# Values of four heads' keys as 64x64 tiles, in two orders, in an attention and gated-MLP kernel

## The chip, the cores and the metric

The kernel runs on one core of a Trainium2 chip. The core has TensorE for matrix products (PE in the profile, its weight loads PEld), VectorE (DVE), ScalarE (ACT) and GpSimd (POOL), each with an instruction queue of its own, and a queue for transfers, SP. Products accumulate in PSUM, everything else is kept in SBUF. The metric is the device time in microseconds; three runs of the kernel before gave a median of 664.06 us (663.80 to 664.94).

## The reference

Eight batches, twelve heads, 448 positions, 64 values a head; the MLP is 768 wide, with 1024 hidden values.

```python
scores = scale * np.matmul(q, k.transpose(0, 1, 3, 2)) - np.log(S)
attn = 1.0 / (1.0 + np.exp(-scores))          # a sigmoid, no sum over keys
x = np.matmul(attn, v)                        # heads side by side: [8, 448, 768]
h = np.maximum(x @ w_in, 0.0)
u, v = h[..., :512], h[..., 512:]
v_n = (v - mean(v)) / sqrt(var(v) + 1e-6)
v_s = einsum('ts,bsd->btd', w_spatial, v_n) + b_spatial[None, :, None]
out = (u * v_s) @ w_out
```

Everything is float32. The kernel makes most products from two halves, a rounded high part and the rest (three products in place of one). The products of the attention with v are made with plain float32 operands, for which the trace shows two matmul instructions each.

## The kernel before

A *unit* is two heads of one batch: 48 units, 12 for each of four passes. A pass `m` (two batches) computes the attention of its units and then the MLP for both batches: gate values `pv` (`gate_values`), spatial products `pg`, hidden values `pu` (`gated`), outputs `po` (`output`). `in_program_order` fixes the order of each engine's instructions to that in which the code emits them, so an instruction that waits holds everything behind it on its engine or queue.

Attention goes by pairs of units, and, from the third pair of pass 0 on, by groups of four units `n` to `n + 3` (`attention_by_fours`): two groups in pass 0, three in each later pass, eleven in all. The 448 keys of a unit are three full tiles of 128 and a short one of 64; the short tiles of two units share one tile. `full` lists the twelve full tiles as (i, t): unit `n + i`, key tile t. Units 0 and 1 of a group write one pair's output, units 2 and 3 the second pair's.

In a group, `score_products` computes each tile's scores into a PSUM place (`banks`: four places of two banks, taken in turn; a score tile's place is that of the fourth one before). A ScalarE sigmoid takes the scores to SBUF; for the tiles in `by_vector`, (0,0), (1,0) and (2,0), a VectorE copy takes them, and ScalarE turns them in place later. Between the tiles the code emits what the next groups need: q/k loads (`attention_loads`), v loads (`value_loads`), and the split of q/k into high and low parts (`attention_splits`: a cast, on ScalarE in pass 0 and on VectorE later, and a VectorE subtraction).

In pass 0 `load_weights(n)` emits the next `n` steps of a generator that loads weights and splits them, mostly on VectorE: ten blocks for the gate and the spatial products must be done when the first gate product needs them. The last three steps make block 5 of `w_g_s`, which the sixth part of each gate product reads. The fours of pass 0 emit 7 steps in the first group and 9 in the second.

Then come the values. `value_products` multiplies a v tile of 128 keys x 64 (weights) with 128 x 448 attention values; the two heads of a unit run side by side, as two 128x64 tiles of the array. The short tiles run as four 64x64 tiles: rows 0 to 63 hold one unit's keys, rows 64 to 127 the other's. The first pair's output leaves PSUM by a ScalarE cast (high part) and a VectorE subtraction (`split_values`, lines 109 and 110). The second pair's is copied by ScalarE to a buffer (line 664), from where VectorE casts it and later subtracts (`lows`, `subtract_lows`). After the values come the short scores of the next group's pairs (line 293).

The buffers: `big` has seven for attention tiles, `vn` and some `gs`; `v` has two, which the v tiles and the second pair's copy share; `tmp` has three.

Of the kernel before, what the change touches and what calls it, by code (L numbers as in the profile page):

```python
# [14 lines left out]
P = 128  # L15
# [20 lines left out]
def attn_gmlp_kernel(  # L36
# [65 lines left out]
    nc.vector.memset(mhalf, -0.5)  # L102

    table = const.tile([P, 1], F32, name="table")
    shift(3 * 32, 2)
    nc.scalar.activation(table, bias_s, AF.Sigmoid)

    def split(hi, lo, src, copy):
        copy(hi, src)  # L109
# [3 lines left out]
        return ps_2.tile([P, 2, 512], F32, tag="ps2", name=name)  # L113


    BIG = 7

    BOUND = 122879.9921875
    SCALE = 2.0**-112
# [166 lines left out]
    def score_products(b, hp, t):  # L286
# [30 lines left out]
                    )  # L317
        return psc[:, :, :S]

    def room(b, hp, t, tag="big"):  # L320
        return work.tile(
            [P, 2, 512], F32, tag=tag, name=f"at_{b}_{hp}_{t}", bufs=BIG if tag == "big" else 3
        )[:, :, :S]

    def attention_scores(b, hp, t):
        psc = score_products(b, hp, t)
# [34 lines left out]
    def attention_values(b, hp, ats, direct):  # L361
        pav = banks(f"pav_{b}_{hp}")
        full = [t for t in range(TILES) if t != NFULL]
        for t in sorted(full, key=lambda t: copied(b, hp, t)) + [NFULL]:
            value_products(pav, b, hp, t, ats(t), start=t in (0, NFULL + 1))
        if direct:
            split_values(pav, b, hp)
        else:
            x = x_of(b, hp)
            xf = work.tile([P, 2, 512], F32, tag="big", name=f"x_{b}_{hp}", bufs=BIG)[:, :, :S]  # L370
# [9 lines left out]

    def warm_up():

        zeros = work.tile([P, 2, 512], F32, tag="big", name="zeros", bufs=BIG)[:, 0, :256]
# [13 lines left out]
    def gate_values(m, ts):  # L397

        n = len(ts)
        pv = banks(f"pv_{m}_{ts[0]}")  # L400
        for i, t in enumerate(ts):
            product(
                pv[:, i, :F],
                [
                    (
                        lambda a, cc=cc, t=t: x_s[:, a, cc, t * P : (t + 1) * P],
                        lambda c, cc=cc: w_g_s[:, cc, c, :],
                    )
                    for cc in range(NCC)
                ],  # L410
            )
        if n > 1:
            load_weights(1 if ts[0] else 5)
        rv = work.tile([P, 2, 512], F32, tag="tmp", name=f"rv_{m}_{ts[0]}", bufs=3)
        nc.scalar.activation(rv[:, :n], pv[:, :n], AF.Relu)  # L415
        mv = work.tile([P, 2, 2], F32, tag="mv", name=f"mv_{m}_{ts[0]}")
        for i in range(n):
            stats = work.tile([P, 6], F32, tag="stats", name=f"stats_{m}_{ts[i]}")
            nc.vector.bn_stats(stats, rv[:, i])  # L419
            nc.vector.bn_aggr(mv[:, i], stats)  # L420
        rstd = work.tile([P, 2], F32, tag="rstd", name=f"rstd_{m}_{ts[0]}")
        nc.gpsimd.tensor_scalar_add(rstd[:, :n], mv[:, :n, 1], 1e-6)
        nc.gpsimd.tensor_tensor(rstd[:, :n], rstd[:, :n], mhalf[:, :n], op=ALU.pow)
        for i in range(n):
            nc.vector.tensor_scalar_sub(rv[:, i], rv[:, i], mv[:, i, 0:1])
        load_weights(n - 1)
        for i, t in enumerate(ts):
            vn = work.tile([P, 2, 512], F32R, tag="big", name=f"vn_{m}_{t}", bufs=BIG)
# [16 lines left out]
            vns[t] = vn  # L445
        if n == 1:
            load_weights(1)
# [62 lines left out]
    def gated(b, fcs):  # L510
# [16 lines left out]
        load_weights(2)  # L527
        nc.vector.scalar_tensor_tensor(g, pu[:, :, :S], 0.0, g, op0=ALU.max, op1=ALU.mult)  # L528
        if odd:
            gs = [  # L530
                work.tile([P, 2, 512], F32R, tag="big", name=f"gs_{b}_{fcs[0]}_{a}", bufs=BIG)[:, :, :S]
                for a in range(2)
            ]
# [54 lines left out]
    def attention_by_fours(m):  # L588
# [9 lines left out]
            shorts[n] = at  # L598

        full = [(i, t) for i in range(4) for t in range(NFULL)]  # L600
        by_vector = [(i, 0) for i in range(3)]
        homes = {by_vector[0]: "wval", by_vector[1]: "tmp"}

        for n in range(first, end, 4):
            if n == first:
                short_scores(n)
# [3 lines left out]
            ats = {}  # L610
# [32 lines left out]
            pavs = [banks(f"pav_{n}_{pair}") for pair in range(2)]  # L643
            order = sorted(full, key=lambda at: (at[0] // 2, at in by_vector))
            begun = set()
            for i, t in order:
                value_products(
                    pavs[i // 2],
                    *units[n + i // 2 * 2],
                    t + i % 2 * (NFULL + 1),  # L650
                    ats[i, t],
                    start=i not in begun,
                )
                begun.add(i)
            for pair in range(2):
                unit = units[n + 2 * pair]
                value_products(pavs[pair], *unit, NFULL, shorts.pop(n + 2 * pair), start=False)
                if pair == 0 or n + 4 == end:
                    split_values(pavs[pair], *unit)
                else:  # L660
                    x = x_of(*unit)
                    xf = work.tile([P, 2 * NFULL + 1, P], F32, tag="v", name=f"x_{n}", bufs=2)
                    xf = xf.rearrange("p a d -> p (a d)").rearrange("p (i s) -> p i s", i=2)
                    nc.scalar.copy(xf, pavs[pair][:, :, :S])
                    nc.vector.tensor_copy(x[:, 0], xf)
                    lows.append((x[:, 1], xf, x[:, 0].bitcast(F32)))
                    ahead(value_loads, n + 4, end)
            for n2 in (n + 4, n + 6):
                if n2 < end:
                    short_scores(n2)  # L670

    def attention(m):

        if m:
            attention_by_fours(m)
            return
# [38 lines left out]
        attention_by_fours(0)  # L715
        w_u.append(const.tile([P, NCC, 2, F], F32R, tag="w_u", name="w_u_s"))

    start_loads(0)
    load_weights(1)
    warm_up()  # L720
    pairs = [(0, 1), (2, 3)]
    for m in range(B // 2):
        attention(m)
        for ts in ((0, 1), (2, 3), (4, 5), (6,)):
            gate_values(m, ts)
        b0, b1 = 2 * m, 2 * m + 1
# [82 lines left out]
```

## Time and profile before

| | us |
|---|---|
| profiled execution | 664.04 |
| its span | 662.3 |
| PE busy | 657.4 (99%) |
| VectorE busy | 317.7 (48%) |
| ScalarE busy | 250.0 (38%) |
| GpSimd busy | 18.5 (3%) |
| value products of the attention (L346), share of the closing chain | 20% |
| scores (L311 and L293), share of the closing chain | 17% |

A row of a timeline gives the start and the length of a run of like instructions, their engine, line, operation, tiles and count, and in brackets the idle time before it and what ended it. A row of groups gives busy time, the mean of one instruction in ns, and the idle time before them. Shapes stand as rows x columns of the array: 128*64 is a tile that takes half of the columns.

### The profile page before, as it was taken

What the parts mean: (1) busy time and instruction counts of PE and PEld (TensorE: products, weight loads), DVE (VectorE), ACT (ScalarE), POOL (GpSimd) and SP (SyncE); (2) the same over time, 40 slices, a digit from 0 to 9 for tenths busy, and PEclk for the clock granted to TensorE, in tenths of its full rate; (3) what the DMA queues carried; (4) which work ended last, traced back from release to release, by engine and by line L of the source; (5) the groups of instructions that cost most, each with busy time, mean ns of one, the idle gap of its engine ahead of it and who ended that gap; (6) DMA issues with size and microseconds to landing.
All of it is one profiled execution on the core that took longest, in us unless ns stands there. A gap on an engine that the chain in (4) does not pass through costs nothing.

```text
span 662.3 us, 8983 instructions
## 1 busy us (share of the span) xinstructions
PE 657.4 (99%) x3830; PEld 506.2 (76%) x3830; DVE 317.7 (48%) x464; ACT 250.0 (38%) x283; POOL 18.5 (3%) x36
## 2 busy tenths in 40 slices
PE   9999999999999999999999999999999999999997
PEld 3645889999755588999965658899986655889997
DVE  4989889842555237132156515613215741652210
ACT  6986322322766510012187641001127872100111
POOL 0000010000000002000000001100000000110000
PEclk9999999999999999999999999999999999999999
DMA  8655213522541310000345050000124510000013
GB/s 296 241 179 189 63 38 106 158 88 83 169 142 56 136 62 0 1 1 28 112 142 169 29 170 27 1 1 0 57 84 142 170 56 0 1 1 0 1 56 111
DMA packets 20695, 55.75 MB, mean 84 GB/s; under 512 B 1968, under 2 KB 8496, under 8 KB 20656
## 3 DMA queue, kind: packets, MB, share of 16 engines
q1 hardware_dynamic: 20368, 54.96, 24.5%
q8 instruction: 30, 0.49, 0.3%
q10 hardware_dynamic: 288, 0.23, 0.1%
q14 instruction: 9, 0.07, 0.0%
HBM read 44.17 MB, written 11.01 MB: 83 GB/s over the span
## 4 chain that ended last, share of the span: by engine, by line
PE 99%; ACT 0%; DVE 0%; issue 0%
PE pav L346 20%; PE po L379 17%; PE pu L379 17%; PE pv L379 17%; PE psc L311 14%; PE pg L491 10%; PE psc L293 3%; PE pg L466 1%; PE warm L388 0%; ACT osb L564 0%; DVE zeros L384 0%; DVE bias_s L100 0%; DVE mhalf L102 0%
## 5 line engine op out<-in xcount | busy, mean ns | idle before, releaser
L275 ACT ACTIVATE at<-psc,bias_s 128x896 f32<-128x896 f32 x129 | 120.3, 1009 | 5.9 <-PE psc L311 4.5
L346 PE MATMUL pav<-at,v 128*64 128x448 f32 (+1 forms) x684 | 120.0, 544 | 0.0
L379 PE MATMUL pu<-x_s,w_u_s 128*128 128x448 f32 x576 | 116.5, 362 | 0.0
L379 PE MATMUL po<-gs,w_out_s 128*128 128x448 f32 x576 | 116.5, 362 | 0.0
L379 PE MATMUL pv<-w_g_s,x_s 128*128 128x512 f32 x504 | 115.4, 390 | 0.0
L379 PEld LDWEIGHTS pu<-x_s,w_u_s 128*128 128x128 f32 x576 | 108.0, 187 | 7.2
L379 PEld LDWEIGHTS po<-gs,w_out_s 128*128 128x128 f32 x576 | 108.0, 187 | 7.2
L379 PEld LDWEIGHTS pv<-w_g_s,x_s 128*128 128x128 f32 x504 | 94.3, 188 | 22.3 <-PE pav L346 2.8
L346 PEld LDWEIGHTS pav<-at,v 128*64 128x64 f32 (+1 forms) x684 | 41.5, 136 | 70.9 <-issue 64.3
L311 PEld LDWEIGHTS psc<-qks 64*128 64x128 f32 x840 | 77.8, 185 | 15.0 <-DVE x_s L110 5.2
L311 PE MATMUL psc<-qks 64*128 64x448 f32 x840 | 88.7, 365 | 0.0
L109 ACT CAST gs<-g 128x896 fp32r<-128x896 f32 x16 | 15.1, 941 | 145.7 <-DVE g L528 145.7
L491 PE MATMUL pg<-w_sp_s,vn 128*128 128x448 f32 x320 | 65.8, 363 | 0.0
L491 PEld LDWEIGHTS pg<-w_sp_s,vn 128*128 128x128 f32 x320 | 59.7, 187 | 5.4 <-issue 1.2
L528 DVE SCALAR_TENSOR_TENSOR g<-pu,g 128x896 f32<-128x896 f32 x16 | 17.4, 1090 | 82.9 <-PE pu L379 82.9
L110 DVE TENSOR_TENSOR x_s<-pav,x_s 128x896 fp32r<-128x896 f32 x16 | 17.1, 1088 | 81.8 <-ACT x_s L109 81.8
L569 ACT COPY osb<-po 128x896 f32<-128x896 f32 x23 | 20.9, 908 | 77.8 <-PE po L379 77.8
L261 DVE TENSOR_TENSOR qks<-raw,qks 128x848 fp32r<-128x848 f32 x46 | 47.4, 1040 | 1.1 <-ACT qks L254 0.2
L415 ACT ACTIVATE rv<-pv 128x1024 f32<-128x1024 f32 (+1 forms) x16 | 14.7, 919 | 75.9 <-PE pv L379 75.9
L419 DVE BATCH_NORM_STATS2 stats<-rv 128x6 f32<-128x512 f32 x28 | 19.0, 679 | 38.3 <-ACT rv L415 38.3
L109 ACT CAST x_s<-pav 128x896 fp32r<-128x896 f32 x16 | 14.1, 909 | 53.9 <-PE pav L346 53.9
L623 DVE COPY wval_s<-psc 128x896 f32<-128x896 f32 x9 | 9.8, 1092 | 47.3 <-PE psc L311 47.3
(61 smaller groups left out, 375.8 us busy)
## 6 DMA issues: line engine op xcount, KB each, us to landing
raw<-qk_dram SPq DMA_DIRECT2D x47, 456.0 KB, 4.9
v<-v_dram SPq DMA_DIRECT2D x24, 448.0 KB, 3.6
out_dram<-osb SPq DMA_DIRECT2D x23, 448.0 KB, 2.6
wraw<-w_in_dram SPq DMA_DIRECT2D x12, 512.0 KB, 6.1
wraw<-w_out_dram SPq DMA_DIRECT2D x6, 512.0 KB, 3.6
wraw<-w_sp_dram SPq DMA_DIRECT2D x4, 256.0 KB, 5.5
raw<-qk_dram SPq DMA_DIRECT2D x1, 296.0 KB, 2.9
b_bc<-b_sp_dram SPq DMA_DIRECT2D x1, 256.0 KB, 5.8
```

Of the source, the lines that this page charges most:

```text
L109: copy(hi, src)
L110: nc.vector.tensor_sub(lo, src, hi.bitcast(F32))
L261: nc.vector.tensor_sub(s[:, 1], loaded[b, hp][:, HALF:], s[:, 0].bitcast(F32))
L275: nc.scalar.activation(at, src, AF.Sigmoid, bias=bias_s, scale=QK)
L293: nc.tensor.matmul(psc[odd * HALF : (odd + 1) * HALF, j, :S], raw[rows, :HALF], raw[rows, HALF + Q :], start=True, stop=True,)
L311: nc.tensor.matmul(psc[:, j, :S], st[rows, k : k + P], mv[rows, Q:PART], start=i == 0, stop=i == len(ops) - 1,)
L346: nc.tensor.matmul(pav[heads, odd, :S], vt[rows, t, heads], at[rows, j], start=start, stop=t == NFULL,)
L379: nc.tensor.matmul(ps, st, mv, start=i == 0, stop=i == len(ops) - 1)
L419: nc.vector.bn_stats(stats, rv[:, i])
L491: nc.tensor.matmul(pg[:, i, :S], st, mv, start=n == 0 and not ended, stop=n == len(ops) - 1 and ended,)
L528: nc.vector.scalar_tensor_tensor(g, pu[:, :, :S], 0.0, g, op0=ALU.max, op1=ALU.mult)
L569: nc.scalar.copy(osb, po[:, :, :S])
```

## The change

1. **Values.** The twelve full tiles of a group are no longer multiplied as 128x64 tiles. `value_steps` multiplies 64 keys of unit a (rows 0 to 63, "low") beside 64 keys of unit c (rows 64 to 127, "high"), four 64x64 matmuls at a time; a second, *swapped* order does the other halves. [...] The steps of both pairs alternate: pair 0 first order, the second pair's short tile and one step, pair 0 swapped, two steps of the second pair, pair 0's short tile, [the next group's first short scores], the second pair swapped.
2. **Vector tiles.** `by_vector` has a fourth tile, (3,0). Its in-place sigmoid and that of (2,0) are emitted behind its scores, followed by the splits of units `n + 4` and `n + 5`. The scores of (3,1) and (3,2) stay in PSUM (`pending`) until the swapped order of pair 0 has been emitted.
3. **Weights in pass 0.** The second group emits 4 steps ahead of the split of unit `n + 6` and 5 behind `split_values` of the first pair; the first group 4 and 3.
4. **Places.** `big` becomes one tile with eight slots taken in turn, and seven slots for the MLP. The second pair's copy goes to a slot, no longer to a v buffer. v loads are emitted behind the last products of their pair; pass 0's first one comes at the start of its first group.
5. **Short scores** of the next group's first pair move ahead of the second pair's swapped steps.

```diff
-        by_vector = [(i, 0) for i in range(3)]
+        by_vector = [(i, 0) for i in range(4)]
...
+                if (i, t) in full[-2:]:
+                    pending.append(((i, t), psc))
+                    continue
...
                     subtract_lows()
-                    if n > first or not m:
-                        ahead(value_loads, n + 2, end)
+                elif (i, t) == by_vector[3]:
+                    for at in by_vector[:1:-1]:
+                        sigmoid(ats[at], ats[at])
+                    for i2 in range(2):
+                        ahead(attention_splits, n + 4 + i2, end)
                 if (i, t) == full[-4]:
                     for at in by_vector[:2]:
                         sigmoid(ats[at], ats[at])
-            sigmoid(ats[by_vector[2]], ats[by_vector[2]])
+            def value_step(i, t, rows):
...
+                for j in range(2):
+                    heads = slice(j * D, (j + 1) * D)
+                    ins = nc.tensor.matmul(
+                        pavs[pair][heads, i % 2, :S],
+                        vt[rows, t if t == NFULL else t + i % 2 * (NFULL + 1), heads],
+                        at[rows, j],
...
+                    if pair in left:
+                        depend(ins, left.pop(pair))
...
+            firsts = [(1, 1), (2, 2), (0, 0)], [(NFULL, NFULL), (1, 0), (2, 1), (0, 2)]
...
+            def value_steps(pair, steps, swapped=False):
+                a, c = 2 * pair, 2 * pair + 1
+                for ta, tb in steps:
+                    if swapped:
+                        value_step(c, tb, low)
+                        ins = value_step(a, ta, high)
+                    else:
+                        value_step(a, ta, low)
+                        ins = value_step(c, tb, high)
+                return ins
+
+            def leave(pair, ins):
+                nc_ins = nc.gpsimd.memset(mark, 0.0).ins
+                depend(nc_ins, ins)
+                left[pair] = nc_ins
+
+            leave(0, value_steps(0, firsts[0]))
+            value_steps(1, firsts[1][:2])
+            leave(0, value_steps(0, firsts[0], swapped=True))
+            for at, psc in pending:
+                ats[at] = slot()
+                sigmoid(ats[at], psc)
             if not m:
-                load_weights(7 if n + 4 < end else 9)
-            for i in range(3):
-                ahead(attention_splits, n + 4 + i, end)
...
+                load_weights(4)
+            ahead(attention_splits, n + 6, end)
+            leave(1, value_steps(1, firsts[1][2:]))
+            value_steps(0, [(NFULL, NFULL)])
+            split_values(pavs[0], *units[n])
+            ahead(value_loads, n + 4, end)
+            if not m:
+                load_weights(3 if n + 4 < end else 5)
+            if n + 4 < end:
+                short_scores(n + 4)
+            value_steps(1, firsts[1][1:], swapped=True)
+            ahead(value_loads, n + 6, end)
...
+                xf = slot()
+                nc.scalar.copy(xf, pavs[1][:, :, :S])
+                nc.vector.tensor_copy(x[:, 0], xf)
+                lows.append((x[:, 1], xf, x[:, 0].bitcast(F32)))
+            if n + 6 < end:
+                short_scores(n + 6)
```

More of the change, by code (lines that the diff above doesn't have):

```diff
@@ L104, in attn_gmlp_kernel, with depend @@
     table = const.tile([P, 1], F32, name="table")
-    shift(3 * 32, 2)
+    mark = const.tile([P, 1], F32, name="mark")
+    shift(2 * 32, 2)
     nc.scalar.activation(table, bias_s, AF.Sigmoid)
+    def depend(ins, on):
+        tc.add_manual_dep(
+            ins,
+            on.name,
+            mybir.DependencyInfo(mybir.DependencyClass.Sync, mybir.DependencyReason.DATA),
+            reason="row tiles of one bank",
+        )
     def split(hi, lo, src, copy):
@@ L113, in banks @@
         return ps_2.tile([P, 2, 512], F32, tag="ps2", name=name)
-    BIG = 7
+    SLOTS = 8
     BOUND = 122879.9921875
@@ L318, in score_products, with slots_of_scores, slots_of_mlp, slot @@
         return psc[:, :, :S]
+    slots = {}
+    def slots_of_scores(m):
+        slots["tile"] = work.tile([P, SLOTS, 2, S], F32, tag="big", name=f"ats_{m}", bufs=1)
+        slots["next"] = 0
+    def slots_of_mlp(m):
+        slots["tile"] = work.tile([P, SLOTS - 1, 2, 512], F32R, tag="big", name=f"mlp_{m}", bufs=1)
+    def slot():
+        n = slots["next"]
+        slots["next"] = (n + 1) % SLOTS
+        return slots["tile"][:, n]
     def room(b, hp, t, tag="big"):
-        return work.tile(
-            [P, 2, 512], F32, tag=tag, name=f"at_{b}_{hp}_{t}", bufs=BIG if tag == "big" else 3
-        )[:, :, :S]
+        if tag == "big":
+            return slot()
+        return work.tile([P, 2, 512], F32, tag=tag, name=f"at_{b}_{hp}_{t}", bufs=3)[:, :, :S]
     def attention_scores(b, hp, t):
@@ L369, in attention_values @@
             x = x_of(b, hp)
-            xf = work.tile([P, 2, 512], F32, tag="big", name=f"x_{b}_{hp}", bufs=BIG)[:, :, :S]
+            xf = slot()
             nc.scalar.copy(xf, pav[:, :, :S])
@@ L381, in warm_up @@
     def warm_up():
-        zeros = work.tile([P, 2, 512], F32, tag="big", name="zeros", bufs=BIG)[:, 0, :256]
+        zeros = slots["tile"][:, SLOTS - 1, 0, :256]
         nc.vector.memset(zeros, 0.0)
@@ L427, in gate_values @@
         for i, t in enumerate(ts):
-            vn = work.tile([P, 2, 512], F32R, tag="big", name=f"vn_{m}_{t}", bufs=BIG)
+            vn = slots["tile"][:, t]
             if t != NFULL:
@@ L529, in gated @@
         if odd:
[L530 to L533, printed above, removed]
+            gs = [slots["tile"][:, fcs[0] + a, :, :S] for a in range(2)]
         else:
@@ L605, in attention_by_fours @@
             if n == first:
+                if not m:
+                    value_loads(*units[n + 2])
                 short_scores(n)
@@ L609, in attention_by_fours @@
                 ahead(attention_loads, n + 4 + i, end)
-            ats = {}
+            ats, pending = {}, []
             for i, t in full:
@@ L637, in attention_by_fours @@
                         sigmoid(ats[at], ats[at])
-            sigmoid(ats[by_vector[2]], ats[by_vector[2]])
-            if not m:
-                load_weights(7 if n + 4 < end else 9)
-            for i in range(3):
-                ahead(attention_splits, n + 4 + i, end)
[L643 to L667, printed above, removed]
@@ L668, in attention_by_fours @@
-            for n2 in (n + 4, n + 6):
-                if n2 < end:
-                    short_scores(n2)
+            pavs = [banks(f"pav_{n}_{pair}") for pair in range(2)]
+            low, high = slice(0, HALF), slice(HALF, P)
+            begun, left = set(), {}
+            def value_step(i, t, rows):
+                pair = i // 2
+                vt = values[units[n + 2 * pair]]
+                at = shorts[n + 2 * pair] if t == NFULL else ats[i, t]
+                for j in range(2):
[4 more added lines that the diff above has]
+                        at[rows, j],
+                        start=i not in begun,
+                        stop=t == NFULL if pair == 0 else (rows == low) == (i % 2) and t == ends[i],
+                    ).ins
+                    if pair in left:
+                        depend(ins, left.pop(pair))
+                begun.add(i)
+                return ins
@@ new lines, in attention_by_fours @@
+            firsts = [(1, 1), (2, 2), (0, 0)], [(NFULL, NFULL), (1, 0), (2, 1), (0, 2)]
+            ends = {2: 0, 3: 2}
+            def value_steps(pair, steps, swapped=False):
[7 more added lines that the diff above has]
+                        ins = value_step(c, tb, high)
+                return ins
@@ new lines, in attention_by_fours @@
+            leave(1, value_steps(1, firsts[1][2:]))
+            value_steps(0, [(NFULL, NFULL)])
+            split_values(pavs[0], *units[n])
+            ahead(value_loads, n + 4, end)
+            if not m:
+                load_weights(3 if n + 4 < end else 5)
[3 more added lines that the diff above has]
+            ahead(value_loads, n + 6, end)
+            unit = units[n + 2]
+            if n + 4 == end:
+                split_values(pavs[1], *unit)
+            else:
+                x = x_of(*unit)
+                xf = slot()
+                nc.scalar.copy(xf, pavs[1][:, :, :S])
+                nc.vector.tensor_copy(x[:, 0], xf)
+                lows.append((x[:, 1], xf, x[:, 0].bitcast(F32)))
@@ L672, in attention @@
+            if n + 6 < end:
+                short_scores(n + 6)
     def attention(m):
+        if m:
+            slots_of_scores(m)
         if m:
@@ L716, in attention @@
         w_u.append(const.tile([P, NCC, 2, F], F32R, tag="w_u", name="w_u_s"))
+    slots_of_scores(0)
     start_loads(0)
@@ L723, in attn_gmlp_kernel @@
         attention(m)
+        slots_of_mlp(m)
         for ts in ((0, 1), (2, 3), (4, 5), (6,)):
```

## The prediction

> **What bounds the kernel now.** I read the page first: the span, then the chain of work that ended last.
>
> ```profile
> span 662.3 us, 8983 instructions
> ...
> PE 99%; ACT 0%; DVE 0%; issue 0%
> ```
>
> The end is set by TensorE alone (PE, with its weight loads PEld); no other engine holds the chain for a whole per cent. So the change can gain only by making the PE stream itself shorter, and it loses wherever it makes PE wait. Next I read the PE timeline and the PEld timeline of one group of four in a later pass, from the end of its values to the next group's values.
>
> ```profile
> 189.24 1.68 PE L293 MATMUL psc<-raw 64*64 64x448 f32 x16
> 190.85 7.48 PE L311 MATMUL psc<-qks 64*128 64x448 f32 x72
> 198.27 3.23 PE L346 MATMUL pav<-at,v 128*64 128x448 f32 x16
> ```
>
> ```profile
> 186.84 0.14 PEld L346 LDWEIGHTS pav<-at,v 128*64 128x64 f32 x2 [0.23 <-issue]
> 187.68 0.21 PEld L346 LDWEIGHTS pav<-at,v 64*64 64x64 f32 x8 [0.70 <-issue]
> 188.11 0.15 PEld L346 LDWEIGHTS pav<-at,v 64*64 64x64 f32 x4 [0.22 <-issue]
> 188.49 0.15 PEld L346 LDWEIGHTS pav<-at,v 64*64 64x64 f32 x4 [0.22 <-issue]
> ```
>
> The loads run one step ahead of the matmuls. A step of 64x64 tiles (four matmuls side by side) takes 188.49 - 188.11 = 0.38 us; across the short scores and into the next line, four such steps (x16) take 190.85 - 189.24 = 1.61 us with the next switch inside. I use 0.376. A step of 128x64 tiles (two side by side) takes the same. From 186.84 to 188.11 lie three steps, 1.13 us, but 1.27 passed: **the switch from 128x64 to 64x64 costs about 0.15 us**. There is one in every group of four. The scores take 0.60 us a tile (7.42 us for twelve and a switch).
>
> **The PE stream after the change.** A full tile was two passes of one 128x64 step; cut into halves it fills, with a half of the other unit, two passes of one 64x64 step. Per group that is 24 + 4 steps before and 28 after: no time removed or added, though matmul instructions go from 64 to 112 (11 groups: 528 more, 3830 to 4358). What goes is the switch inside the values: 11 x 0.15 = **-1.65 us**. The switch from 64x128 scores to 64x64 values has no row of this kind before; it may cost what the present one to 128x64 costs, or, as the row halves stay, nothing, which would save 0.14 x 11 = 1.5 us more. I take the full price, since the way back from 64x64 to 64x128 is not free: 1.61 less four steps leaves 0.11. [...]
>
> **The ordered swaps.** GpSimd must see the last matmul of one order, do a 128x1 memset, and release PE's next order.
>
> ```profile
> L422 POOL TENSOR_SCALAR rstd<-mv 128x1 f32<-128x1 f32 x4 | 2.1, 520 | 14.2 <-DVE mv L420 14.2
> L793 POOL MEMSET const-bfloat16-1.0<- 128x1 bf16 x1 | 0.1, 103 | 0.0
> ```
>
> From the start of a step to an engine it releases pass about 0.62 us (worked out below), then 0.10 for the memset and 0.1 to a weight load: 0.82. Other work of the queue lies between: five steps, 1.88 us, or three, 1.13 us, in the last group of a pass, which has no short scores to put there. So it is hidden. If the memset took the 0.52 of the other row, 1.24 against 1.13 would cost 0.1 in each of four passes: between 0 and +0.4; I take 0. Nothing else of GpSimd's is queued in attention.
>
> **An earlier need of the second vector tile.** Tile (1,0), which ScalarE turns in place, was used by the eleventh and twelfth step of the values; now it is in the fifth, 0.43 + 3 x 0.376 = 1.55 us after the values start.
>
> ```profile
> 198.76 1.04 ACT L275 ACTIVATE at<-at,bias_s 128x896 f32<-128x896 f32 x1
> ```
>
> It ends at 199.80, 1.53 after 198.27; with 0.05 to the weight load and 0.05 for a load that nothing hides (0.43 - 0.376), PE goes on at 1.63: +0.08, at most, in each group. The postponed tiles (3,1) and (3,2) follow without a wait: their slots come free as the first two swapped tiles end, ScalarE needs 1.0 us for each, and by the same 0.62 and 0.05 they are ready 0.1 to 0 us ahead of their steps. Their late eviction holds only two score places that no product wants before the short scores. Together 11 x 0.07 = +0.8, between 0 and +0.9.
>
> **v loads and the copy through a slot.**
>
> ```profile
> v<-v_dram SPq DMA_DIRECT2D x24, 448.0 KB, 3.6
> ```
>
> A v load now waits on the SP queue for the products alone, with q/k loads and, in pass 0, weight loads behind it; it lands in 3.6 us and the next values begin some 10 us later: nothing. The copy to a slot costs what the copy to a v buffer did.
>
> **Pass 0, where the queues turn against PE.** Here the casts of units 8 to 10 run on ScalarE, and VectorE also prepares weights. The first group's values start at 35.04.
>
> ```profile
> 35.04 3.23 PE L346 MATMUL pav<-at,v 128*64 128x448 f32 x16
> ...
> 47.38 7.51 PE L311 MATMUL psc<-qks 64*128 64x448 f32 x72
> 54.82 3.23 PE L346 MATMUL pav<-at,v 128*64 128x448 f32 x16
> ...
> 65.65 28.88 PE L379 MATMUL pv<-w_g_s,x_s 128*128 128x512 f32 x126
> ```
>
> ```profile
> 36.47 2.80 ACT L275 ACTIVATE at<-psc,bias_s 128x896 f32<-128x896 f32 x3
> 39.14 1.06 ACT L275 ACTIVATE at<-at,bias_s 128x896 f32<-128x896 f32 x1
> 40.08 2.51 ACT L254 CAST qks<-raw 128x848 fp32r<-128x848 f32 x3
> ```
>
> ```profile
> 33.30 0.42 DVE L190 CAST w_g_s<-wval_s 128x512 fp32r<-128x512 f32 x1
> ...
> 38.27 0.43 DVE L190 CAST w_g_s<-wval_s 128x512 fp32r<-128x512 f32 x1
> ...
> 42.27 2.96 DVE L261 TENSOR_TENSOR qks<-raw,qks 128x848 fp32r<-128x848 f32 x3
> 46.20 1.09 DVE L110 TENSOR_TENSOR x_s<-pav,x_s 128x896 fp32r<-128x896 f32 x1 [0.97 <-ACT x_s L109]
> 47.21 0.62 DVE L665 CAST x_s<-x 128x896 fp32r<-128x896 f32 x1
> ```
>
> Before, VectorE did seven weight steps from 33.30 to 42.27 while ScalarE finished its sigmoids, and took the subtractions for units 8 to 10 only when their casts had been made. The change puts the subtractions for units 8 and 9 ahead of all seven. ScalarE, free of tile (1,0) at 36.47, now turns (3,0) and (2,0) in place (0.94 each, 39.14 to 40.08), and only then casts unit 8: 38.35 to 39.27. **VectorE, done with its copy of (3,0) at about 35 (its scores end some 1.1 us before 35.04, and a copy takes 1.1), waits there until 39.3, over 4 us.** Then, in its order: two subtractions (0.95 each) to 41.2; four weight steps, 38.27 - 33.30 = 4.97, to 46.2; unit 10's subtraction to 47.1; the first pair's (1.09) to 48.2. The wait list shows what hangs on that one:
>
> ```profile
> PEld psc L311 <- DVE x_s L110: 5.2, 8, 0.7
> ```
>
> The next group's first score tile takes the PSUM place that this subtraction frees. It would start at 47.3 (47.38 less 0.15, plus 0.08); it starts at 48.3: +0.95. Next on VectorE stand the three other weight steps (3.5 us, from 55.50 to 59.02 below), to 51.6, the cast of the second pair, 0.55, to 52.2, and only now the copy of score tile (0,0), to 53.3. The fifth score tile needs that place and would start at 50.8 (four tiles of 0.60 and the switch after 48.3); it starts at 53.35 with 0.1 of weight load in the open: +2.6. VectorE then keeps up, so the second group's values start at 54.82 + 0.95 + 2.6 - 0.07 = 58.3.
>
> ```profile
> 54.06 0.68 DVE L129 SCALAR_TENSOR_TENSOR wval_s<-wraw,wval_s 128x512 uint32<-128x512 uint32 x1
> ...
> 55.50 0.43 DVE L190 CAST w_g_s<-wval_s 128x512 fp32r<-128x512 f32 x1
> ...
> 59.02 0.69 DVE L129 SCALAR_TENSOR_TENSOR wval_s<-wraw,wval_s 128x512 uint32<-128x512 uint32 x1
> ...
> 64.38 0.43 DVE L190 CAST w_g_s<-wval_s 128x512 fp32r<-128x512 f32 x1
> 64.84 0.69 DVE L191 TENSOR_TENSOR w_g_s<-wval_s,w_g_s 128x512 fp32r<-128x512 f32 x1
> ```
>
> ```profile
> 65.04 1.72 ACT L109 CAST x_s<-pav 128x896 fp32r<-128x896 f32 x2 [5.08 <-PE pav L346]
> ```
>
> Before, the last five weight steps ran from 59.02 to 65.53, ahead of the pair's subtraction. Now the first pair's subtraction stands ahead of them. The pair ends with step 22, which starts at 58.3 + 0.43 + 20 x 0.376 + 0.08 = 66.33. (Before, the pair's last step stood three steps and a switch of 0.11 ahead of 65.65, at 64.42, and the cast began at 65.04: the 0.62 used above.) So the cast runs from 66.95 to 67.86, the subtraction to 68.9, and the five steps after it: high half of the last gate weight at 68.9 + (64.38 + 0.43 - 59.02) = 74.7, low half at 75.4. PE has six more steps, starts the gate product at 66.33 + 7 x 0.376 + 0.11 = 69.07, and reaches the last sixth of its first tile (15 products of 0.23, 28.88/126, and 0.1) at 72.6. **It waits until 74.8, then 0.25 more for the low half: +2.45.** Pass 0 in all: 69.07 - 65.65 + 2.45 = +5.9 us. TensorE has no idle time later to take that back.
>
> **The sum**, against the profiled execution's own 664.04 (1.74 more than its span; the median of the runs is 664.06): pass 0 +5.9 with its two groups' savings in it; nine later groups 9 x (-0.15 + 0.07) = -0.7. 664.04 + 5.2 = **669.2 us**. Its own range, from the free switch (-1.5) to the slow memset (+0.4) and a microsecond of error in the chain of pass 0, is 667.7 to 670.7.
>
> **Rivals.**
>
> *The waits of pass 0 don't reach PE.* Then the removed switch decides: 664.04 - 1.65 + 0.8 = 663.2, or 662.4 where the fifth step doesn't wait. For it: VectorE is 48% busy over the span, and the change splits the weight steps in two so that the pair's subtraction comes sooner. Against it: each engine follows its written order, and the rows put unit 8's cast behind four in-place sigmoids. It decides if VectorE frees the pair's bank by 47.3 and ends the last gate weight by about 69.
>
> *Only one of the two waits bites.* The last gate weight alone: 663.2 + 2.45 = 665.6; the held score places alone: 663.2 + 3.55 = 666.7. For it: the margins of the first group (0.95 of 4 us) are thin and hang on ScalarE's order. Against it: the two have different causes.
>
> *TensorE's queue can't feed four small tiles.* The scores run 72 matmuls and 72 loads in 7.42 us, 51.5 ns each; a 64x64 step has eight in 0.376, 47 ns. If 51.5 were a limit, each step would take 0.412: 28 x 9 x 0.036 = 9.1 us in the later passes and 1 to 2 in pass 0: 679 to 680. Against it: eight 64x64 steps in a row (187.68 to 190.85) already keep 0.376, but 64 instructions can have been queued ahead. [...]
>
> *The tiles don't run side by side*, because low and high rows stream from different score tiles: two steps for one, 10 us a group, 780 in all. Against it: the short scores already take four streams from two different tiles (L293) at 0.376.
>
> **How the numbers follow.** A measurement of this kernel can tell about 0.2%, 1.33 us: faster is below 662.7, slower above 665.4. I give the forecast 0.64, the first rival 0.15 (a third of it below 662.7), one wait alone 0.14, the queue 0.05, serial tiles 0.02. Slower: 0.64 + 0.14 + 0.07 less a little for the lower end of the one-wait case, 0.82; the first rival's two thirds and that little, 0.13; faster 0.05. The range takes in the forecast's own and the one-wait cases: 665.2 to 671.0.
>
> **What would show it.** Right: PE x4358; no step of 0.8 between value loads; in the window 46 to 54 a weight load for scores waiting about 1 us for x_s of VectorE and another about 2.6 us for the copy of a score tile; VectorE idle about 4 us near 35 to 39, released by ScalarE's cast; the gate product's first tile waiting over 2 us for w_g_s; later groups 0.1 us shorter. Wrong: the gate product starting near 65.5 and running on, or 64x64 steps longer than 0.38 in long runs.

## The result and the profile after

The changed kernel takes 672.17 us, median of five runs (670.84 to 672.37), beside 664.06 us before: a ratio of the means of 1.0115, 95% interval 1.01 to 1.0129. It is slower, as forecast, but by 8.1 us where 5.2 were forecast, and 1.2 us outside the range. Left out of every median and ratio here are three executions that took over twice the usual time, two of e6_fill_both (1728 us) and one of the kernel before (1338.68 us).

The head of the page of the changed kernel; its profiled execution took 672.37 us:

```profile
span 670.6 us, 10096 instructions
...
PE 660.7 (99%) x4358; PEld 530.0 (79%) x4358; DVE 329.8 (49%) x475; ACT 252.9 (38%) x283; POOL 21.8 (3%) x69
...
PE 94%; DVE 3%; ACT 2%; issue 1%; ACTq 0%
```

The matmul count is the predicted 4358. The chain that ended last was PE alone before; now VectorE and ScalarE hold 5% of it: somewhere TensorE waited for them. The list of waits of the changed kernel between 24 and 103 us (engine, tile and line, what was waited for: us in total, times, longest) says where:

```profile
PE psc L320 <- DVE places L648: 2.2, 1, 2.2
PE pv L402 <- DVE w_g_s L199: 1.9, 1, 1.9
...
PE psc L320 <- DVE x_s L119: 0.7, 1, 0.7
...
PEld pav L676 <- POOL mark L703: 0.3, 1, 0.3
```

Three waits stop the matmuls themselves (the PE rows): 0.72 us for the first pair's subtraction (x_s), 2.24 us for the copy of a score tile (places), 1.94 us for the high half of the last gate weight (w_g_s). GpSimd's mark, set between the two orders of a pair, holds back a weight load for 0.3 us, but no matmul; no run leaves the mark out, so that the orders have to be kept apart is not shown. From 178 us on no matmul waits for another engine.

The timeline of VectorE in the changed kernel shows the cause, in the order in which its queue holds it:

```profile
39.42 1.99 DVE L270 TENSOR_TENSOR qks<-raw,qks 128x848 fp32r<-128x848 f32 x2 [4.20 <-ACT qks L263]
...
47.14 1.08 DVE L119 TENSOR_TENSOR x_s<-pav,x_s 128x896 fp32r<-128x896 f32 x1
...
52.06 1.08 DVE L648 COPY places<-psc 128x896 f32<-128x896 f32 x1
...
69.38 1.09 DVE L119 TENSOR_TENSOR x_s<-pav,x_s 128x896 fp32r<-128x896 f32 x1 [4.49 <-ACT x_s L118]
```

VectorE stands idle for 4.20 us until ScalarE's cast (39.42). Its later work is late by that: the first pair's subtraction starts at 47.14 (46.20 before), the copy of the score tile at 52.06, and behind the subtraction at 69.38 come the last five weight steps.

Now the PE timeline, from the second group's scores to the next pass; two rows of before follow, which the prediction does not show:

```profile
48.28 2.67 PE L320 MATMUL psc<-qks 64*128 64x448 f32 x24 [0.72 <-DVE x_s L119]
53.20 6.67 PE L320 MATMUL psc<-qks 64*128 64x448 f32 x48 [2.24 <-DVE places L648]
59.80 1.74 PE L676 MATMUL pav<-ats,v 64*64 64x448 f32 x16
...
70.58 3.70 PE L402 MATMUL pv<-w_g_s,x_s 128*128 128x512 f32 x15
76.22 27.31 PE L402 MATMUL pv<-w_g_s,x_s 128*128 128x512 f32 x111 [1.94 <-DVE w_g_s L199]
103.37 4.17 PE L514 MATMUL pg<-w_sp_s,mlp 128*128 128x448 f32 x20
...
178.34 1.73 PE L302 MATMUL psc<-raw 64*64 64x448 f32 x16
```

```profile
94.37 4.17 PE L491 MATMUL pg<-w_sp_s,vn 128*128 128x448 f32 x20
...
169.36 1.73 PE L293 MATMUL psc<-raw 64*64 64x448 f32 x16
```

One row does not fit a wait that costs its length: 48 score products take 6.67 us, 0.139 each, where all 72 took 7.51 before, 0.104 each. The granted clock is the share of TensorE's full speed that the profile says it was given. These are the stretches of the changed kernel in which the slow products stand (stretch, its length, PE busy and instructions, granted clock, DMA share, GB/s):

```profile
50.07:53.48 3.41, 1.17 (x12) 1.00 0.47 139
53.48:56.89 3.41, 3.41 (x22) 0.50 0.38 152
...
73.96:77.37 3.41, 1.47 (x6) 1.00 0.00 0
77.37:80.78 3.41, 3.41 (x10) 0.50 0.00 0
```

**After each of the two longer waits TensorE runs, in this execution, one stretch of 3.41 us at half clock.** The two stretches start 77.37 - 53.48 = 23.89 us apart, seven times 3.41. The work of half such a stretch, 1.7 us, comes later, and with TensorE 99% busy it stays lost. That is in no term of the prediction.

### The profile page after: what moved, and what is told of

Read it like the earlier page. It is cut to its first block, busy times and chain, and to the rows that moved or that the text cites. A ratio compares the mean times of both kernels' runs of the same rounds, so it can differ in the third digit from the quotient of the medians.

```text
span 670.6 us, 10096 instructions
## 1 busy us (share of the span) xinstructions
PE 660.7 (99%) x4358; PEld 530.0 (79%) x4358; DVE 329.8 (49%) x475; ACT 252.9 (38%) x283; POOL 21.8 (3%) x69
## 4 chain that ended last, share of the span: by engine, by line
PE 94%; DVE 3%; ACT 2%; issue 1%; ACTq 0%
PE po L402 17%; PE pu L402 17%; PE pv L402 17%; PE pav L676 16%; PE psc L320 13%; PE pg L514 10%; PE psc L302 3%; PE pav L369 2%; ACT ats L284 1%; PE pg L489 1%; PE warm L411 0%; DVE qks L270 0%; DVE x_s L119 0%; DVE w_g_s L200 0%; DVE wval_s L138 0%
## 5 line engine op out<-in xcount | busy, mean ns | idle before, releaser
L284 ACT ACTIVATE ats<-psc,bias_s 128x896 f32<-128x896 f32 x100 | 93.6, 1007 | 26.4 <-PE pav L676 15.3
L676 PE MATMUL pav<-ats,v 64*64 64x448 f32 x880 | 93.6, 539 | 0.0
L676 PEld LDWEIGHTS pav<-ats,v 64*64 64x64 f32 x880 | 43.7, 133 | 36.6 <-issue 20.2
L514 PE MATMUL pg<-w_sp_s,mlp 128*128 128x448 f32 x320 | 65.8, 363 | 0.0
L514 PEld LDWEIGHTS pg<-w_sp_s,mlp 128*128 128x128 f32 x320 | 59.7, 188 | 5.4 <-issue 1.2
L402 PE MATMUL po<-gs,w_out_s 128*128 128x448 f32 x288 | 58.9, 362 | 0.0
L402 PE MATMUL po<-mlp,w_out_s 128*128 128x448 f32 x288 | 58.3, 362 | 0.0
L402 PEld LDWEIGHTS po<-mlp,w_out_s 128*128 128x128 f32 x288 | 54.0, 188 | 3.6
L402 PEld LDWEIGHTS po<-gs,w_out_s 128*128 128x128 f32 x288 | 54.0, 188 | 3.6
L118 ACT CAST gs<-g 128x896 fp32r<-128x896 f32 x8 | 7.5, 942 | 96.1 <-DVE g L551 96.1
```

The costliest lines, as they stand in the source:

```text
L284: nc.scalar.activation(at, src, AF.Sigmoid, bias=bias_s, scale=QK)
L402: nc.tensor.matmul(ps, st, mv, start=i == 0, stop=i == len(ops) - 1)
L514: nc.tensor.matmul(pg[:, i, :S], st, mv, start=n == 0 and not ended, stop=n == len(ops) - 1 and ended,)
L676: ins = nc.tensor.matmul(pavs[pair][heads, i % 2, :S], vt[rows, t if t == NFULL else t + i % 2 * (NFULL + 1), heads], at[rows, j], start=i ...
```

## The experiments

Diffs are against the changed kernel unless another is named; ratios are of means, against runs of before from the same session (medians 664.08 to 664.25). The granted clock of a run is its mean: one half-clock stretch lowers it by 0.5 x 3.41/670 = 0.0025, to 0.997, two to 0.995. The changed kernel's runs say the same: 672.17 to 672.37 us at 0.995, 670.84 and 671.15 at 0.997.

### Taking the two late pieces back, one by one

**e1_weights_back**: the second group of pass 0 makes all nine weight steps ahead of the first pair's subtraction, as before.

```diff
-                load_weights(4)
+                load_weights(4 if n + 4 < end else 9)
...
-                load_weights(3 if n + 4 < end else 5)
+                load_weights(3 if n + 4 < end else 0)
```

> Only pass 0's second group is changed back: all nine weight steps stand ahead of the first pair's subtraction again. Theory (two waits of TensorE in pass 0, each followed by one 3.4 us stretch in which the granted clock is 0.5): the wait for the last gate weight goes, 2.1 to 2.4 us, and with it the second stretch, 1.7 us: 672.2 - 4.0 = 668.2, granted clock about 0.997. Rival (the waits alone cost, and the slow stretch behind them has another cause that stays, such as VectorE being late): 672.2 - 2.3 = 669.9. Rival (the 64x64 steps with their guards are dearer everywhere): no change worth naming, 671 to 672.

**e2_splits_back**: in pass 0 the splits of units n + 4 and n + 5 go back behind the values, and the first group's seven weight steps stand ahead of its first pair's subtraction.

```diff
-                    for i2 in range(2):
+                    for i2 in range(2 if m else 0):
                         ahead(attention_splits, n + 4 + i2, end)
...
-                load_weights(4)
-            ahead(attention_splits, n + 6, end)
+                load_weights(7 if n + 4 < end else 4)
+            for i2 in range(2 if m else 0, 3):
+                ahead(attention_splits, n + 4 + i2, end)
...
-                load_weights(3 if n + 4 < end else 5)
+                load_weights(0 if n + 4 < end else 5)
```

> Only pass 0's first group is changed back: seven weight steps, then the splits of units n+4 to n+6, all ahead of the first pair's subtraction; the second group stays as in the changed kernel. Theory: VectorE does not wait near 35 to 39, the two waits of the scores near 47 to 53 (0.8 and 2.2 us) shrink to 0.3 at most, and the half-clock stretch behind them (1.7 us) goes: 672.2 - 4.5 = 667.7. Rival (clock stretch has another cause): 672.2 - 2.8 = 669.4. Rival (tiles dearer everywhere): 671 to 672.

**e3_both_back**: both edits; the values, tiles, slots and swaps of the change stay.

> Both of the two edits together; the 64x64 values, the ordered swaps, the postponed tiles and the slots all stay. Theory: what is left is the removed switch less the wait for tile (1,0): 663.2 to 663.7, granted clock 0.999 as in the kernel before, no idle time of TensorE in pass 0 beyond 0.3. Rival (tiles and guards dearer): 665 or more.

| | median us (range) | ratio to before, 95% interval |
|---|---|---|
| e1_weights_back | 668.57 (666.70 to 668.59) | 1.0060, 1.0048 to 1.0073 |
| e2_splits_back | 666.49 (665.97 to 667.69) | 1.0039, 1.0027 to 1.0052 |
| e3_both_back | 663.31 (662.75 to 664.01) | 0.9988, 0.9979 to 0.9997 |

The PE timelines of e1, of e2 and of e3, in this order:

```profile
53.49 6.67 PE L320 MATMUL psc<-qks 64*128 64x448 f32 x48 [2.24 <-DVE places L648]
...
70.87 28.86 PE L402 MATMUL pv<-w_g_s,x_s 128*128 128x512 f32 x126
```

```profile
47.62 7.51 PE L320 MATMUL psc<-qks 64*128 64x448 f32 x72
...
65.82 3.69 PE L402 MATMUL pv<-w_g_s,x_s 128*128 128x512 f32 x15
71.46 27.36 PE L402 MATMUL pv<-w_g_s,x_s 128*128 128x512 f32 x111 [1.94 <-DVE w_g_s L199]
98.66 4.17 PE L514 MATMUL pg<-w_sp_s,mlp 128*128 128x448 f32 x20
```

```profile
47.36 7.49 PE L320 MATMUL psc<-qks 64*128 64x448 f32 x72
...
65.55 28.86 PE L402 MATMUL pv<-w_g_s,x_s 128*128 128x512 f32 x126
```

Each edit removes its own wait and leaves the other as it was (2.24 in e1, 1.94 in e2), so the two have the two causes that the prediction named. With both gone the time is just below that of before: the slowdown lay in the order of pass 0 alone. (e2 takes back the early splits and the 4-and-3 division of the weight steps together; their shares of its two waits are not separated.) e1 and e3 came out within 0.4 us of what was expected; the median of e2 is 1.2 us below its 667.7, because three of its five runs kept the whole clock behind the wait that was left in. The runs of e2 also price the stretch: 667.6 and 667.7 us at 0.997, 666.0 to 666.5 at 1.0, so **about 1.5 us for one half-clock stretch**. In e1 four runs at 0.996 to 0.997 take 668.5 to 668.6, the one at 0.999 takes 666.70. The medians of e1 and e2 thus depend on how many runs caught the stretch.

### Keeping TensorE busy while it waits

If the lost clock comes from TensorE's idle time, products that are thrown away should keep it, with every wait in place.

**e5_busy_wait** does it for the last wait, on top of e2:

```diff
+            if fill is not None and i == 15:
+                for _ in range(FILL):                      # 9
+                    nc.tensor.matmul(fill, ops[0][0], ops[0][1], start=True, stop=True)
             nc.tensor.matmul(ps, st, mv, start=i == 0, stop=i == len(ops) - 1)
...
+                fill=pv[:, 1, :F] if (m, t) == (0, 0) else None,
```

> The second kernel of this call (splits back in the first group, weights still late in the second) with nine products more, whose results are thrown away, put ahead of the sixteenth product of the first gate tile, where TensorE waits for the last gate weight: 9 x 0.23 = 2.06 us of matmuls in a wait of about 2.1. Theory (idle time makes the granted clock fall to 0.5 for 3.4 us): TensorE has no idle stretch, the clock stays, and nine products more make the kernel faster by 1.7 than the same one without them: about 666.0. Rival (the slow products behind the wait come from late data or from VectorE): the same time as without them or up to 0.3 more, 667.7 to 668.0.

It took 666.54 us (665.89 to 667.03), ratio 1.0035 (1.0023 to 1.0048); no run fell below a clock of 0.999. Its PE timeline:

```profile
65.01 3.70 PE L407 MATMUL pv<-w_g_s,x_s 128*128 128x512 f32 x15
68.55 2.20 PE L406 MATMUL pv<-w_g_s,x_s 128*128 128x512 f32 x9
...
96.22 4.17 PE L520 MATMUL pg<-w_sp_s,mlp 128*128 128x448 f32 x20
...
101.49 0.68 PE L495 MATMUL pg<-w_sp_s,mlp 64*128 64x448 f32 x3 [0.29 <-ACT rv L444]
```

From the first gate product to the first spatial product pass 96.22 - 65.01 = 31.21 us, in the profiled run of e2 98.66 - 65.82 = 32.84: the filler brought 1.63. But the median equals that of e2, because three of e2's five runs had kept their clock anyway. In e5 a new wait also stands behind (101.49), taken up below; whether those three runs of e2 have it too is not shown, since e2's profile is of a run at 0.997.

**e6_fill_both** does it for both longer waits, in the changed kernel itself: the nine products, and 44 of 64 columns into columns of the fourth score tile that nothing reads.

```diff
+            for f in range(fill):                          # 44 in the second group, tile (1, 0)
+                rows = slice(f % 2 * D, (f % 2 + 1) * D)
+                nc.tensor.matmul(
+                    psc[:, f % 2, S : S + D],
+                    ops[0][0][rows, k : k + P],
+                    ops[0][1][rows, Q : Q + D],
+                    start=True,
+                    stop=True,
+                )
```

> The changed kernel with every wait of pass 0 left where it is, but with products that are thrown away put into the two long ones: 44 products of 64 columns, into the unused columns of the fourth score tile of the second group, ahead of the fifth tile, and nine of 512 columns, into the unused half of the first gate tile, ahead of its 16th product. TensorE is then busy while it waits, and nothing else is earlier. Theory (a wait of about 2 us costs its length, and about 1.7 us more in the half-clock stretch that follows it): the changed kernel's 672.2 less two times 1.7 = 668.8, between 668.2 and 669.4, and no run with a mean granted clock below 0.998. Rival (the half clock is not set off by TensorE's idle time, or what it costs lies elsewhere): 670.8 to 672.4, as the changed kernel, with the clock at 0.995 to 0.997.

It took 670.22, 670.31 and 670.70 us, all at a clock of 1.0; the ratio is 1.0095 (1.0079 to 1.011). Both expectations missed: the clock was kept, but only 2 us came back instead of 3.4. So two more runs asked where the rest had gone.

**e6_fill_24**: 24 in place of the 44 products.

> As e6_fill_both, with 24 products in place of 44 ahead of the fifth score tile. Theory: the 44 took longer than the wait that they were to fill, and the clock was kept; with 24 the wait for the copied score tile shows again, under 1 us, both waits are too short for a half-clock stretch, and the time is 668.8 (668.2 to 669.4). Rival (the waits cost their length and 1.5 us more each, whatever the clock does): 670.2 to 670.7, as with 44.

**e6_fill_44**: the kernel of e6_fill_both again, with a profile (670.18 us, span 668.4).

> e6_fill_both again, for a profile of it. Theory: the 44 products end about 1.5 us behind the copy of the score tile for which the fifth one waits (53.2 in the changed kernel's profile), no stretch stands at half clock, and the rest of pass 0 follows 1.5 us later than that copy allows. Rival: the products end by 53.2, and the 1.5 us lie elsewhere.

The PE timeline of e6_fill_44:

```profile
48.58 2.68 PE L320 MATMUL psc<-qks 64*128 64x448 f32 x24 [0.73 <-DVE x_s L119]
51.10 2.54 PE L329 MATMUL psc<-qks 64*128 64x64 f32 x44
53.51 5.08 PE L320 MATMUL psc<-qks 64*128 64x448 f32 x48
58.52 1.73 PE L691 MATMUL pav<-ats,v 64*64 64x448 f32 x16
...
69.30 3.70 PE L416 MATMUL pv<-w_g_s,x_s 128*128 128x512 f32 x15
...
100.51 4.17 PE L529 MATMUL pg<-w_sp_s,mlp 128*128 128x448 f32 x20
...
105.76 0.68 PE L504 MATMUL pg<-w_sp_s,mlp 64*128 64x448 f32 x3 [0.27 <-ACT rv L453]
...
176.18 1.74 PE L302 MATMUL psc<-raw 64*64 64x448 f32 x16
```

The theory that the 44 products ran too long falls: the fifth score tile follows 53.51 - 48.58 = 4.93 us after the first, in the changed kernel 53.20 - 48.28 = 4.92. What follows is shorter: 48 score products in 5.08 us instead of 6.67. Stage by stage, in differences of starts, this kernel beside before, the changed kernel and the prediction:

| stage of TensorE | before | changed, against before | predicted | e6_fill_44, against before |
|---|---|---|---|---|
| second pass-0 group: first scores, from the first group's values | 12.34 | +0.73 | +0.92 | +0.71 |
| its scores, to its values | 7.44 | +4.08 | +2.56 | +2.50 |
| its values, to the gate product | 10.83 | -0.05 | -0.06 | -0.05 |
| gate product, to the spatial products | 28.72 | +4.07 | +2.45 | +2.49 |
| from there to pass 1 | 74.99 | -0.02 | 0 | +0.68 |
| passes 1 to 3 | 492.94 | -0.68 | -0.7 | -0.72 |

(The first values of all start 0.2 us later than before in the changed kernel and 0.5 later in e6_fill_44.) **With the clock kept, both stages take what the prediction gave them, within 0.06 us**; the half-clock stretches are the +1.5 and +1.6 on top. Of the 3.2 us that the fillers bring, 0.7 are given back in the row below: at 105.76 the spatial products wait for ScalarE's rv, which takes the last gate tile out of PSUM (the matmuls stand idle for 0.27 us, a weight load ahead of them for 0.6). ScalarE's timeline in e6_fill_44 shows why: this rv starts at 105.12, right behind a weight's cast (line 214, 104.59) that had waited 3.86 us for a weight step of VectorE (line 141). It comes 2.2 us earlier than in the changed kernel (107.29), the spatial products 2.9 us, so there the slow stretch had hidden the wait. No run took the weight steps away.

With 24 products, e6_fill_24 took 670.18 and 670.29 us in the runs at 1.0, and 671.43 and 671.95 at 0.996: the same as 44 products when the clock holds, 1.2 to 1.7 us more when it doesn't. Its expectation, that the shortened wait would never cost the clock, missed.

### One wait in several lengths

On top of e3, where TensorE has no wait in these stages, VectorE makes the high half of the last gate weight 10, 13 or 17 times over (w_short, w_mid, w_long).

```diff
+            for _ in range(13 if n == NFIRST - 1 else 1):
                 nc.vector.tensor_copy(hi, val)
```

> The kernel with both edits back, and VectorE's copy to the high half of the last gate weight made ten times in place of once (nine copies of 0.36 to 0.46 us more; the result is the same). The weight was ready some 3.1 us before TensorE's sixteenth gate product, so TensorE waits 0.2 to 1.0 us there. Theory (a stretch of about 3.4 us falls to half clock only if TensorE idles through more than about half of the one before): the clock stays whole in every run, 663.3 + 0.2 to 1.0 = 663.5 to 664.3. Rival (any idle time of TensorE brings the half clock): 1.7 more, 665 to 666, granted clock 0.997.

> The same with thirteen copies (twelve more): TensorE waits 1.2 to 2.4 us. Theory: some of the runs keep the whole clock and some lose 1.7 us, as the stretch borders fall, with a granted clock of 0.997 in just those: 664.5 to 665.7 or 666.2 to 667.4. Rival (the half clock follows from late VectorE work, not from TensorE's idle time): all runs alike.

> The same with seventeen copies (sixteen more): TensorE waits 2.7 to 4.3 us. Theory: every run loses one stretch of 3.4 us at half clock, granted clock 0.997 in each: 663.3 + 2.7 to 4.3 + 1.7 = 667.7 to 669.3. Rival (no link to the length of the idle time): the clock as in the shorter waits.

| | TensorE's wait | us, median (range) | clock of the five runs |
|---|---|---|---|
| w_short | 0.93 | 666.49 (666.17 to 667.54) | 1.0, 1.0, 0.997, 0.999, 1.0 |
| w_mid | 2.31 | 667.49 (667.37 to 668.32) | 0.997, 0.999, 0.997, 0.997, 0.997 |
| w_long | 4.17 | 669.69 (669.14 to 670.43) | 0.997, 0.997, 0.995, 0.997, 0.995 |

The three waits lie in the ranges expected for them, but all three medians lie above theirs, and w_short was expected to keep the clock in every run. In its profile the gate product, up to the spatial products, takes 30.20 us in place of e3's 28.70, so that a wait of 0.93 us cost 1.5 at the whole clock, and a second wait of 1.3 us stands behind, again for rv. (So a kept clock need not show in the time: the run of w_mid at 0.999 took 667.49 us, those at 0.997 from 667.37.) What they do show is the step of the clock: it is kept in four of five runs, lost in four, lost in all. (Which of its two waits cost w_short's one run the clock is not shown; the two runs of w_long at 0.995 have, by that clock, lost two stretches; they have no profile.) The stretches of w_short, w_mid and w_long, and of e6_fill_24:

```profile
68.53:71.94 3.41, 2.48 (x10) 1.00 0.00 0
```

```profile
68.65:72.06 3.41, 1.13 (x5) 1.00 0.00 0
72.06:75.47 3.41, 3.38 (x8) 0.50 0.00 0
```

```profile
66.99:70.41 3.42, 2.31 (x11) 1.00 0.00 0
70.41:73.82 3.41, 0.35 (x2) 1.00 0.00 0
73.82:77.23 3.41, 3.41 (x9) 0.50 0.00 0
```

```profile
50.63:54.05 3.42, 2.43 (x36) 1.00 0.63 161
54.05:57.46 3.41, 3.41 (x22) 0.50 0.32 129
```

I cut the time into stretches of 3.41 us from each run's own clock changes. With whole-size products, the stretches in which TensorE was busy for 2.14 (w_short's wait for rv, 99.25 to 102.66: 3.41 less the 1.27 of that wait), 2.31 or 2.48 us (0.9 to 1.3 idle) were followed by the whole clock, those with 1.65 (e2, 69.70 to 73.11), 1.47, 1.17, 1.13 or 0.35 by half. The one that breaks the row, e6_fill_24 with 2.43, is filled with 64-column products; why it lost the clock is not shown. The rows follow not the length of a wait but how much of it falls into one stretch, and the stretches lie differently in each profiled run: one starts 1.20 us ahead of the wait for the gate weight in w_short (68.53, the wait from 69.73), 0.32 ahead of it in the changed kernel (73.96, 74.28), 0.18 behind its start in e2 (69.70, 69.52). That would explain why the same kernel loses the clock in some runs only; the runs without a profile don't show it.

### The order of the values

**e4_reorder**: the splits as in e3, six and ten weight steps instead of seven and nine, and tile (1,0) wanted 0.75 us later (two steps of 0.376).

```diff
-            leave(0, value_steps(0, firsts[0]))
-            value_steps(1, firsts[1][:2])
+            value_steps(0, firsts[0][:2])
+            value_steps(1, firsts[1][:1])
+            leave(0, value_steps(0, firsts[0][2:]))
+            value_steps(1, firsts[1][1:2])
```

> Pass 0 as in the kernel before (splits behind the weight steps, six steps in the first group and ten in the second, all ahead of the first pair's subtraction), and in each group the second pair's short tile is put ahead of the first pair's third step, so that tile (1,0) is wanted 0.75 us later. Theory: the wait of about 0.05 to 0.1 us for tile (1,0) goes in eleven groups, and 0.15 in pass 0: 663.3 - 0.8 = 662.5, against 664.1 to 664.2 of the kernel before. Rival (the guard over GpSimd, now with three steps between in place of five, becomes the wait): 663.3 or more, with loads waiting for the mark.

It took 663.56 us (662.94 to 663.94), ratio 0.9989 (0.9981 to 0.9998): a miss by a microsecond. In its profile the eight short spatial products of pass 0 take 1.46 us (98.66 to 100.12), 1.07 in e3 (98.35 to 99.42). **e7_order** is the same order of the values with seven and nine steps, that is e3 with the diff above and nothing else.

> The kernel with 7 and 9 weight steps and all splits ahead of the first pair's subtraction, and the value steps in the order of e4_reorder (tile (1,0) needed one step later). By the later passes of e4_reorder, 0.07 to 0.1 us a pass shorter than e3_both_back: 663.31 - 0.3 = 663.0, between 662.6 and 663.4. If the new order gains nothing: 663.3 to 663.6.

It took 662.78 us (662.44 to 663.07), ratio 0.998 (0.9971 to 0.9989), the fastest of all. The start of pass 2 in the timelines of before and of the changed kernel (pass 1 starts at 169.36 and 178.34, above), and both starts in that of e7:

```profile
332.47 1.73 PE L293 MATMUL psc<-raw 64*64 64x448 f32 x16
```

```profile
341.16 1.73 PE L302 MATMUL psc<-raw 64*64 64x448 f32 x16
```

```profile
169.09 1.74 PE L302 MATMUL psc<-raw 64*64 64x448 f32 x16
...
331.82 1.74 PE L302 MATMUL psc<-raw 64*64 64x448 f32 x16
```

Pass 1 takes 163.11 us before, 162.82 in the changed kernel, 162.81 in e3 (169.23 to 332.04) and 162.73 in e7. So a group of the change is shorter by about 0.1 us, and the later need of tile (1,0) adds 0.03, not the 0.07 that I had put on its wait. The first values of e7's profiled run started early, at 10.15, so its lead over e3 (the intervals overlap) is not shown to be more than these 0.1 us a pass.

## Why the prediction was wrong

**Right: the order of the queues in pass 0.** VectorE's idle time (4.20 us, "over 4"), its release by ScalarE's cast (39.42, forecast 39.3), the first pair's subtraction (47.14 to 48.22, forecast 47.1 to 48.2) and the score tile's copy (to 53.14, forecast 53.3) came as worked out; the last gate weight let TensorE go on 5.64 us after the gate product's start, forecast 5.7. The three waits are there, 0.72, 2.24 and 1.94 us, for the terms 0.95, 2.6 and 2.2. e1 and e2 show their causes, e3 that nothing else was slow.

**Right: the later passes.** -0.68 us for -0.7, with the switch gone, tile (1,0) in time, the guards and the v loads hidden: no matmul waits there. The pieces within -0.7 were a little off: the early need of (1,0) is 0.03 by e7 rather than 0.07. The full price of the switch from 64x128 to 64x64 was the right end: had it been free, a group would have gained 0.15 us more. Twelve score tiles with the switch behind them take 7.40 us in the changed kernel (199.65 to 207.05), 7.42 before. Two slips in the sum change nothing: 48.2 + 3.5 makes 51.7, not 51.6, and the microsecond of error was counted at the upper end of the range only.

**Wrong: the step from a wait to its price.** "It waits until 74.8", "+2.45", and "+0.95", "+2.6" were added as if TensorE came back from a wait at full speed. It came back at half the clock for 3.41 us, twice: +1.5 and +1.6 us. 669.2 and these 3.1 make 672.3, the profiled execution 672.37. No rival and no bound held it; the range was built from errors of the chain. The trace of before has no row for it: its matmuls wait for no engine after the start-up, so what follows a wait had no price in it, and a term without a row was set to zero without being named.

**The rivals.** That the waits don't reach TensorE, or one only, fell with the list of waits. The queue that can't feed four small tiles and the tiles that don't run side by side fell too: in the later passes six steps of 64x64 tiles take 198.74 - 196.48 = 2.26 us, 0.376 each, as before. Before, eight such steps in a row (eight instructions each, 64) kept 0.376, which left open whether they had been queued ahead; here 32 in a row (256 instructions: 28 steps of values, four of short scores) take 199.65 - 187.41 = 12.24 us, 0.38 each with the switch to the scores in it.

```profile
187.41 1.73 PE L676 MATMUL pav<-ats,v 64*64 64x448 f32 x16
...
196.48 2.48 PE L676 MATMUL pav<-ats,v 64*64 64x448 f32 x24
198.74 0.98 PE L302 MATMUL psc<-raw 64*64 64x448 f32 x8
199.65 7.47 PE L320 MATMUL psc<-qks 64*128 64x448 f32 x72
```

**Still open** are what lies between the stretches of 3.41 us that were idle for 1.3 and kept the clock and the one idle for 1.8 that lost it (whole-size products), why the stretch with 24 short products lost it, and how much of the wait for rv would be left without weight steps on VectorE and ScalarE.

## What to carry to other kernels

A wait put on the bounding engine can cost more than its length (here 2.24 and 1.94 us cost 1.5 and 1.6 more): ask what clock it comes back with, and add that term or name it as unknown, above all where the trace before has no such wait to read it from. Moving work ahead in an in-order queue moves every wait of that work ahead too: here two subtractions put before seven weight steps made VectorE idle 4 us, and the gain of the new values, under 0.1 us a group, was lost several times over. Keep such a change to the passes where the moved work has its inputs; the values of this change with the old order of pass 0 beat both kernels, by 0.1 to 0.2% the one before.

## What was not expected of the hardware

- One wait of TensorE of 1.94 us was enough for 3.41 us at half clock, about 1.5 us lost, in two of e2's five runs; w_short, with 0.93 us and a second wait of 1.3, kept the clock in four of five, w_long, with 4.17 us, in none.
- Products thrown away into the wait keep the clock (e5, e6_fill_both and e6_fill_44, in all nine runs that count), and then the two waits cost what the prediction put on them, within 0.06 us. 24 short products in place of 44 kept it in two runs of four.
- The slow stretch after one wait can hide the next: with the clock kept, 0.7 of 3.2 us turned into a wait for rv.
